# One batch's Newton steps on another engine, and tiles moved within the memory, in a fused attention and two-MLP kernel

## The chip, the cores and the metric

The kernel runs on one core of a Trainium2 chip. The metric is the device time of one execution in microseconds (us), from the first to the last instruction and what lies around it. Three executions of the kernel before took 1564.74, 1565.35 and 1567.13 us; their median is 1565.35 us.

## The reference

Three stages follow one another. Linear attention over 8 batches of 8 heads with 576 positions, each head divided by its root mean square; then an MLP with a cosine gate; then an MLP whose two halves are multiplied.

```python
kv  = einsum('bhsd,bhse->bhde', k, v)
out = einsum('bhsd,bhde->bhse', q, kv)
out = out / sqrt(mean(out * out, -1) + 1e-6) * g_norm
x = out laid out as 4608 tokens x 512
h = x @ w_in                  # 512 -> 2048
x = (h * cos(h)) @ w_out      # 2048 -> 512
h = ((x @ w1) * (x @ w2)) @ w3
y = h @ w_out                 # 1024 -> 512
```

Everything is float32. The kernel keeps the precision by splitting each operand into a high and a low part and multiplying three times (high by high, high by low, low by high).

## The kernel before

**Units.** The attention is cut into 16 units of 288 positions, two to a batch. A unit needs, for each of four pairs of heads, a split of q into high and low (`emit_qs`, tile `hl`: the high half on ScalarE, the low half on VectorE for units 0 to 3 and on GpSimd from unit 4 on, see `small`), three matmuls (`emit_out`), and two reads of the result out of PSUM. Then come the mean squares (`emit_ms`) and the inverse root: `emit_rs` writes the sums to DRAM and reads them back into 128 x 18 (tile `rsx`), `emit_newton` finds the root with a seed and three Newton rounds, 11 small instructions on VectorE, `emit_bc` writes it to DRAM and reads it back spread over the partitions (tile `bc`, one buffer), and `emit_x` multiplies. For units 2 and 3 (the second batch) all these transfers are issued from GpSimd's queue (`queue`); for the later units from SyncE's.

**First MLP.** Tokens go in blocks of 512. A step n multiplies a block with one of 16 weight pairs: `emit_h` (12 matmuls, PSUM tile `h`), the gate (`g_first`, `g_rest`: ScalarE and VectorE in turns, tile `g`), and two steps later `emit_w` (12 matmuls into tile `x`). Steps 0 to 7 take block 0, which needs units 0 and 1; step 8 starts block 1, which needs units 1, 2 and 3. So units 2 and 3 are worked out while steps 0 to 6 run (the table `quick`), and while the weights that arrive are unpacked on VectorE and ScalarE (`bits`, `Pair`). Later units are spread over later steps (`unit_stage`).

**Second MLP.** `emit_wc` folds two weight matrices into one (tile `wc`), then chains of products with 384 columns (tiles `X`, `V`, `Y`, line 790) and the output matmuls with 512 columns (`emit_o`, tile `o`) run to the end.

**Order.** The instructions of an engine start in a fixed order. A planner sets that order when the program is built, from the order of the code, the dependences and a simulated timeline, and pulls work forward where an engine seems free: in the trace units 4 and 5 are worked on from 83 us, far ahead of the steps that they are written beside. `tc.issue_after(ins)` puts every instruction of its block that is on the engine of `ins` behind `ins` in that order.

**Where tiles lie.** A partition's memory is filled from both ends. On the left, in this order, are the pools `const` (`kv0` to `kv3`, `sel`, `gneg`, `spread`), `mlp` (rows, x, g) and `attn`, later `mlp2` (wo2, wc). On the right, down from the top at byte 221152, lie the weights, later the pool `right` (xc, w12, ab, some of wo2). In the program before, `spread` takes 384 bytes at byte 20768, the pool `mlp` begins at byte 21152, x at 31392 and g at 47776; weight 0 begins at 212960. All these operands have sizes and inner offsets that are multiples of 512 bytes where TensorE reads them, so two numbers describe them: 160, the place of the left ones within 512 bytes, and 480, that of the right ones. In `emit_h`, `emit_w` and `emit_o` the operand that streams through (512 columns) lies on the left and the stationary one on the right. In `emit_wc` the stationary one lies on the left, and the streaming one on the left for c below 4 and on the right from c = 4 on. In line 790 both lie on the right.

Of the kernel before, what the change touches and what calls it, by code (L numbers as in the profile page):

```python
# [7 lines left out]
F32 = mybir.dt.float32  # L8
F32R = mybir.dt.float32r
I32 = mybir.dt.int32  # L10
AF = mybir.ActivationFunctionType
ALU = mybir.AluOpType

P = 128
EPS = 1e-6
# [5 lines left out]
RSQRT_SEED = float(0x5F3759DF)  # L21
HUGE = 3.0e38
# [7 lines left out]
def f32(ap):  # L30
    return ap.bitcast(F32)
# [3 lines left out]
def kernel(  # L35
# [18 lines left out]
    nc = tc.nc  # L54
    B, NPAIR, NHALF, _, HALF = qt.shape
# [10 lines left out]
    RS = 2 * NPAIR * HALF // P  # L66

    const = ctx.enter_context(tc.tile_pool(name="const", bufs=1))
    wstack = ExitStack()
    wpool = wstack.enter_context(tc.tile_pool(name="weights", bufs=1, side="right"))  # L70
    dram = ctx.enter_context(tc.tile_pool(name="scratch", bufs=1, space=bass.MemoryType.DRAM))
# [5 lines left out]
    ap = attn.enter_context(tc.tile_pool(name="attn", bufs=1))  # L77
# [11 lines left out]
    load = {"vector": 0.0, "pool": 0.0, "alone": True}  # L89

    def even(n):

        if load["alone"]:
            return nc.vector
        v, g = load["vector"] + 60 + n * 1.05, load["pool"] + 100 + n * 1.8
        if v <= g:
            load["vector"] = v
            return nc.vector
        load["pool"] = g
        return nc.gpsimd  # L100

    def split(dst, src, lo_engine=None):

        nc.scalar.activation(dst[:, 0], src, AF.Copy)  # L104
        lo_engine = lo_engine or even(src.shape[-1])
        lo_engine.tensor_tensor(dst[:, 1], src, f32(dst[:, 0]), ALU.subtract)  # L106
# [174 lines left out]
    def queue(u):  # L281

        return nc.gpsimd if 2 <= u < 4 else nc.sync

    def small(u):
        return None if u < 4 else nc.gpsimd

    q_raw = {}
# [9 lines left out]

    def emit_qs(u, p):
        hl = ap.tile([P, 2, HALF], F32R, tag="hl", bufs=2, name=f"qhl_{u}_{p}")  # L300
        split(hl, q_raw.pop((u, p)), small(u))
        q_hl[p] = hl

    o_sb = {}
# [44 lines left out]
    def newton(x, y, t):  # L349

        nc.vector.tensor_scalar(
            y.bitcast(I32), x.bitcast(I32), -0.5, RSQRT_SEED, ALU.mult, ALU.add
        )
        for _ in range(3):
            nc.vector.tensor_tensor(t, x, y, ALU.mult)
            nc.vector.scalar_tensor_tensor(t, t, 0.5, y, ALU.mult, ALU.mult)
            end = nc.vector.scalar_tensor_tensor(y, t, 1.5, y, ALU.subtract, ALU.mult)
        return end

    def emit_newton(u):  # L360

        x = rs[u]
        y, t = (
            ap.tile([P, RS], F32, tag=f"rs{i}", bufs=2, name=f"rs{i}_{u}") for i in range(2)
        )
        load["vector"] += 1000
        nc.vector.tensor_scalar(x, x, EPS, HUGE, ALU.add, ALU.min)
        newton(x, y, t)
        rs[u] = y

    bc = {}

    def emit_bc(u):
        y = rs.pop(u)
        d = dram.tile([2 * NPAIR, HALF], F32, tag="rsd", bufs=2, name=f"rsd_{u}")
        queue(u).dma_start(out=d.rearrange("h s -> (h s)").rearrange("(p f) -> p f", f=RS), in_=y)
        t = ap.tile([P, NPAIR, HALF], F32, tag="bc", name=f"bc_{u}")
        rows = d.rearrange("(p h) s -> h p s", h=2)
        for h in range(2):
            queue(u).dma_start(out=t[64 * h:64 * h + 64], in_=rows[h].partition_broadcast(64))  # L380
        bc[u] = t

    def emit_x(u, p):
# [6 lines left out]
    T3 = HALF // NT3  # L390
# [81 lines left out]
    def unit_stage(u, s, newton=NEWTON, last=LAST):  # L472
# [16 lines left out]
        if 1 <= s <= NPAIR:  # L489
            late.append(lambda: emit_qs(u, s - 1))  # L490
# [6 lines left out]
        if s == newton:  # L497
            late.append(lambda: emit_newton(u))
            late.append(lambda: emit_bc(u))
# [387 lines left out]
    if True:  # L887
# [5 lines left out]
        nc.gpsimd.memset(sel, 0.0)  # L893
        for h in range(2):
            nc.gpsimd.memset(sel[D * h:D * h + D, h:h + 1], 1.0 / D)
        spread = const.tile([P, T3], F32, name="spread")
        nc.gpsimd.memset(spread, 0.0)
        nc.gpsimd.affine_select(
            out=spread, in_=spread, compare_op=ALU.not_equal, fill=1.0, base=0,
# [12 lines left out]
        for h in range(2):  # L912
            nc.sync.dma_start(
                out=gneg[D * h:D * h + D], in_=g_norm.rearrange("(d o) -> d o", o=1)
# [32 lines left out]
        for n in range(NS + 2):  # L947
            t, m, first, last = steps[n] if n < NS else (NB, n - NS, False, False)
# [171 lines left out]
        h, g = order[-1]  # L1120
# [63 lines left out]
```

## Time and profile before

| what | value |
|---|---|
| median of three executions | 1565.35 us |
| the profiled execution | 1564.83 us |
| its span, first to last instruction | 1563.0 us |
| TensorE busy | 1517.0 us (97%), 7616 matmuls |
| VectorE, ScalarE, GpSimd busy | 921.4, 694.0, 370.9 us |
| mean granted TensorE clock | 0.991 of full speed |

The profile is of one execution. A matmul's end is modelled, so the rate at which matmuls follow each other is read from their starts. Times inside the trace count from the first instruction; 1.8 us lie outside the span.

### The profile page before, as it was taken

How to read it: one execution, taken by the hardware profiler on the slowest of the kernel's cores; microseconds unless marked ns; L12 is line 12 of the kernel's file. 1: busy time of each engine (PE TensorE's matmuls, PEld its weight loads, DVE VectorE, ACT ScalarE, POOL GpSimd, SP SyncE). 2: the span in 40 equal slices, each digit the busy share in tenths (PEclk: the TensorE clock that was granted, in tenths of full speed). 3: DMA queues.
4: the chain of work that ended last, by engine and by line, in shares of the span. 5: the costliest groups of instructions: out<-in, count | busy, mean ns of one | idle time of the engine just before them, and what ended most of it. 6: DMA issues, size and time to landing. Idle time of an engine off the chain costs nothing.

```text
span 1563.0 us, 20358 instructions
## 1 busy us (share of the span) xinstructions
PE 1517.0 (97%) x7616; PEld 1271.9 (81%) x7616; DVE 921.4 (59%) x1639; ACT 694.0 (44%) x1375; POOL 370.9 (24%) x301
## 2 busy tenths in 40 slices
PE   6887999999999999999999998999999999999998
PEld 6665888777787787777878786989998898999997
DVE  4986774567566676656665546745434456545453
ACT  5665554444444454444534335443333334333331
POOL 1121020011010121101102005464344416444420
PEclk9898999999999999999999999999999999999999
DMA  9653020433423424334222106121112313233312
GB/s 347 217 175 88 0 78 21 147 99 94 123 85 122 128 96 132 97 118 132 84 65 81 46 0 229 41 68 68 44 65 82 108 37 116 75 111 121 122 60 75
DMA packets 79794, 156.24 MB, mean 100 GB/s; under 512 B 11360, under 2 KB 37136, under 8 KB 77776
## 3 DMA queue, kind: packets, MB, share of 16 engines
q1 hardware_dynamic: 78080, 150.18, 29.3%
q0 software_dynamic: 1616, 4.78, 0.9%
q8 instruction: 59, 0.97, 0.3%
q14 instruction: 39, 0.32, 0.1%
HBM read 113.77 MB, written 41.15 MB: 99 GB/s over the span
## 4 chain that ended last, share of the span: by engine, by line
PE 82%; DMA 6%; POOL 4%; DVE 3%; ACT 2%; issue 2%; SPq 1%; ACTq 0%; DVEq 0%; POOLq 0%
PE X L790 10%; PE h L555 8%; PE h L556 8%; PE h L557 8%; PE x L557 8%; PE x L556 8%; PE x L555 8%; PE V L790 5%; PE o L555 4%; PE o L556 4%; PE o L557 4%; PE Y L790 2%; POOL xc L106 2%; DMA x2r<-x_all 2%; DMA words<-in_w1pair_dram 2%
## 5 line engine op out<-in xcount | busy, mean ns | idle before, releaser
L790 PE MATMUL X<-xc,w 128*128 128x384 f32 x1152 | 229.5, 337 | 6.5 <-ACT s L798 5.8
L556 PE MATMUL x<-g,w 128*128 128x512 f32 x576 | 229.4, 398 | 1.1 <-DVE g L106 1.1
L557 PE MATMUL x<-g,w 128*128 128x512 f32 x576 | 229.2, 398 | 0.0
L555 PE MATMUL h<-x,w 128*128 128x512 f32 x544 | 219.2, 404 | 9.7 <-DVE u L583 5.0
L790 PEld LDWEIGHTS X<-xc,w 128*128 128x128 f32 x1152 | 203.7, 188 | 20.3 <-ACT s L798 9.9
L556 PE MATMUL h<-x,w 128*128 128x512 f32 x544 | 217.9, 400 | 0.0
L557 PE MATMUL h<-x,w 128*128 128x512 f32 x544 | 217.3, 399 | 0.0
L555 PE MATMUL x<-g,w 128*128 128x512 f32 x576 | 210.5, 397 | 2.5 <-ACT g L104 2.5
L106 POOL TENSOR_TENSOR xc<-x2r,xc 128x768 fp32r<-128x768 f32 x70 | 133.3, 1911 | 227.3 <-ACT xc L104 227.3
L569 ACT ACTIVATE u<-h 128x512 f32<-128x512 f32 x144 | 86.1, 598 | 178.7 <-PE h L557 175.4
L582 ACT ACTIVATE u<-u 128x512 f32<-128x512 f32 x144 | 90.8, 631 | 115.6 <-DVE u L578 104.0
L106 DVE TENSOR_TENSOR g<-u,g 128x512 fp32r<-128x512 f32 x144 | 103.8, 721 | 63.8 <-ACT g L104 63.5
L104 ACT ACTIVATE g<-u 128x512 fp32r<-128x512 f32 x144 | 91.0, 632 | 101.3 <-DVE u L583 75.3
L555 PEld LDWEIGHTS h<-x,w 128*128 128x128 f32 x544 | 103.5, 191 | 39.6 <-DVE u L583 8.7
L556 PEld LDWEIGHTS x<-g,w 128*128 128x128 f32 x576 | 108.8, 189 | 27.9 <-DVE g L106 1.9
L577 DVE TENSOR_SCALAR r<-u 128x512 f32<-128x512 f32 x112 | 51.1, 456 | 136.3 <-ACT u L569 135.9
L555 PEld LDWEIGHTS x<-g,w 128*128 128x128 f32 x576 | 107.6, 188 | 28.1 <-ACT g L104 2.9
L557 PEld LDWEIGHTS x<-g,w 128*128 128x128 f32 x576 | 108.8, 189 | 25.8
L106 POOL TENSOR_TENSOR qhl<-q,qhl 128x288 fp32r<-128x288 f32 x48 | 43.1, 900 | 360.3 <-ACT qhl L104 293.5
L798 ACT ACTIVATE s<-X 128x384 f32<-128x384 f32 x144 | 65.9, 487 | 134.0 <-PE X L790 133.8
L583 DVE TENSOR_TENSOR u<-u,h 128x512 f32<-128x512 f32 x144 | 98.4, 683 | 44.5 <-ACT u L582 44.1
L557 PEld LDWEIGHTS h<-x,w 128*128 128x128 f32 x544 | 103.6, 191 | 24.5 <-issue 0.5
(185 smaller groups left out, 2629.4 us busy)
## 6 DMA issues: line engine op xcount, KB each, us to landing
x2r<-x_all SPq DMA_DIRECT2D x44, 384.0 KB
words<-in_w1pair_dram SPq DMA_DIRECT2D x15, 1024.0 KB
kvraw<-in_kv_main_dram SPq DMA_DIRECT2D x28, 512.0 KB
x_all<-x2s SPq DMA_DIRECT2D x36, 256.0 KB
part<-o SPq DMA_DIRECT2D x36, 256.0 KB
part<-part SPq DMA_DIRECT2D x36, 256.0 KB
out_dram<-part SPq DMA_DIRECT2D x36, 256.0 KB
d_w<-in_w12w_dram SPq DMA_DIRECT2D x16, 512.0 KB
```

What stands on the lines that cost most here:

```text
L104: nc.scalar.activation(dst[:, 0], src, AF.Copy)
L106: lo_engine.tensor_tensor(dst[:, 1], src, f32(dst[:, 0]), ALU.subtract)
L555: nc.tensor.matmul(ps, w[0], x[0], start=first, stop=False)
L556: nc.tensor.matmul(ps, w[0], x[1], start=False, stop=False)
L557: nc.tensor.matmul(ps, w[1], x[0], start=False, stop=last)
L569: nc.scalar.activation(u, h_ps[n], AF.Identity, bias=0.25, scale=INV_2PI)
L577: nc.vector.tensor_scalar(r, u, ROUND, ROUND, ALU.add, ALU.subtract)
L582: nc.scalar.activation(u, u, AF.Sin, scale=-TWO_PI_DOWN)
L583: nc.vector.tensor_tensor(u, u, h_ps.pop(n), ALU.mult)
L790: nc.tensor.matmul(ps, w[:, self.i, a, k], x[:, b, k], start=first and k == 0 and n == 0, stop=last and k == 1 and n == 2, skip_group_chec ...
L798: nc.scalar.activation(s, ps, AF.Copy)
```

## The change

The Newton steps of units 2 and 3 move from VectorE to GpSimd. `newton_on_gpsimd` spells out in 13 instructions what took 10, as the fused form (two operations with two tensors) is split; with the clamp in `emit_newton` it is 14 instead of 11. The low halves of units 4 and 5 are put behind the last transfer of unit 3's spreading in GpSimd's order. `spread` moves from the pool `const` into the slot of `bc`, which leaves the left side 384 bytes shorter ahead of the pool `mlp`. A tile of 48 floats that nothing reads or writes is placed first on the right side, so that all behind it lies 192 bytes lower.

```diff
     const = ctx.enter_context(tc.tile_pool(name="const", bufs=1))
+
+    shift = ctx.enter_context(tc.tile_pool(name="shift", bufs=1, side="right"))
+    shift.tile([P, 48], F32, name="shift")
@@
-        split(hl, q_raw.pop((u, p)), small(u))
+        with tc.issue_after(spreads[0].ins) if u in (4, 5) else nullcontext():
+            split(hl, q_raw.pop((u, p)), small(u))
@@
+    def newton_on_gpsimd(x, y, t):
+        nc.gpsimd.tensor_scalar(
+            y.bitcast(I32), x.bitcast(I32), -0.5, RSQRT_SEED, ALU.mult, ALU.add
+        )
+        for _ in range(3):
+            nc.gpsimd.tensor_tensor(t, x, y, ALU.mult)
+            nc.gpsimd.tensor_tensor(t, t, y, ALU.mult)
+            nc.gpsimd.tensor_scalar(t, t, 0.5, -1.5, ALU.mult, ALU.add)
+            nc.gpsimd.tensor_tensor(y, t, y, ALU.mult)
@@
-        load["vector"] += 1000
-        nc.vector.tensor_scalar(x, x, EPS, HUGE, ALU.add, ALU.min)
-        newton(x, y, t)
+        engine = nc.vector
+        if 2 <= u < 4:
+            engine = nc.gpsimd
+        else:
+            load["vector"] += 1000
+        engine.tensor_scalar(x, x, EPS, HUGE, ALU.add, ALU.min)
+        (newton if engine is nc.vector else newton_on_gpsimd)(x, y, t)
@@
+        if u == 3:
+            spreads.append(op)
@@
-        spread = const.tile([P, T3], F32, name="spread")
+        spread = ap.tile([P, T3], F32, tag="bc", name="spread")
```

## Rows read from the trace of the kernel before

**Rows 1.** The page's first line.

```profile
span 1563.0 us, 20358 instructions
```

**Rows 2.** Busy time by stretch: PE, PEld, DVE, ACT, POOL, granted clock, DMA.

```profile
100.00:150.00 50.00, 36.67 (x167) 25.20 (x166) 31.66 (x81) 28.12 (x64) 10.57 (x14) 0.83 0.41 124
150.00:250.00 100.00, 100.00 (x429) 80.38 (x428) 69.73 (x97) 56.91 (x91) 8.50 (x8) 1.00 0.13 39
```

**Rows 3.** Chain that ended last, in order of time: start us, us, what.

```profile
93.44 4.98 DMA msd<-ms_sb
...
98.97 4.58 DMA rsx<-msd
...
121.42 4.55 DMA bc<-rsd
```

**Rows 4.** Timeline of DVE: start us, us, instruction, idle before and its releaser.

```profile
98.97 0.17 DVE L356 SCALAR_TENSOR_TENSOR rs<-rs,rs 128x18 f32<-128x18 f32 x1
103.57 0.18 DVE L367 TENSOR_SCALAR rsx<-rsx 128x18 f32<-128x18 f32 x1 [4.43 <-DMA rsx<-msd]
...
104.98 0.17 DVE L357 SCALAR_TENSOR_TENSOR rs<-rs,rs 128x18 f32<-128x18 f32 x1
...
126.00 1.56 DVE L386 TENSOR_TENSOR o<-o,bc 128x288 f32<-128x288 f32 x4 [6.47 <-DMA bc<-rsd]
```

**Rows 5.** Timeline of POOL, the same columns.

```profile
24.34 0.19 POOL L419 TENSOR_TENSOR gate<-sq 128x1 f32<-128x1 f32 x1 [21.83 <-ACT sq L413]
...
83.12 0.98 POOL L106 TENSOR_TENSOR qhl<-q,qhl 128x288 fp32r<-128x288 f32 x1 [4.24 <-ACT qhl L104]
89.40 3.51 POOL L106 TENSOR_TENSOR qhl<-q,qhl 128x288 fp32r<-128x288 f32 x1 [5.30 <-DVE rs L355]
92.85 1.18 POOL L345 DMA_DIRECT2D msd<-ms_sb  x2
...
118.46 0.59 POOL L376 DMA_DIRECT2D rsd<-rs  x1 [0.70 <-DVE rs L357]
120.81 1.23 POOL L380 DMA_DIRECT2D bc<-rsd  x2 [1.77 <-DMA rsd<-rs]
...
135.03 0.81 POOL L106 TENSOR_TENSOR qhl<-q,qhl 128x288 fp32r<-128x288 f32 x1 [4.18 <-ACT qhl L104]
```

**Rows 6.** Timeline of PE where block 1 begins.

```profile
126.88 1.22 PE L555 MATMUL h<-x,w 128*128 128x512 f32 x2 [2.49 <-ACT x L104]
...
141.58 0.50 PE L555 MATMUL h<-x,w 128*128 128x512 f32 x1 [4.86 <-DVE u L583]
```

**Rows 7.** Timeline of PE, first MLP: streaming left, stationary right.

```profile
750.09 0.40 PE L555 MATMUL x<-g,w 128*128 128x512 f32 x1
...
755.69 0.40 PE L555 MATMUL x<-g,w 128*128 128x512 f32 x1
```

**Rows 8.** Timeline of PE, `emit_wc` with c below 4: both on the left.

```profile
948.87 0.39 PE L555 MATMUL wc<-wo,w3hl 128*128 128x512 f32 x1
...
954.31 0.39 PE L555 MATMUL wc<-wo,w3hl 128*128 128x512 f32 x1
```

**Rows 9.** Timeline of PE, `emit_wc` with c from 4: streaming right, stationary left.

```profile
992.71 0.39 PE L555 MATMUL wc<-wo,w3hl 128*128 128x512 f32 x1
...
995.46 0.33 PE L790 MATMUL X<-xc,w 128*128 128x384 f32 x1
```

**Rows 10.** Timeline of PE, line 790: both on the right, 384 columns.

```profile
1007.26 2.24 PE L790 MATMUL X<-xc,w 128*128 128x384 f32 x12
1009.34 1.20 PE L790 MATMUL Y<-xc,w 128*128 128x384 f32 x6
```

**Rows 11.** PE by line, 150 to 1005 us: count, busy us, mean ns, idle before.

```profile
L557 PE MATMUL x<-g,w 128*128 128x512 f32 x543 | 215.3, 397 | 0.0
...
L557 PE MATMUL h<-x,w 128*128 128x512 f32 x497 | 196.5, 395 | 0.0
...
L557 PE MATMUL h<-x_again,w 128*128 128x512 f32 x32 | 12.7, 396 | 0.0
```

**Rows 12.** PE by line, 1005 to 1563 us, the same columns.

```profile
L790 PE MATMUL X<-xc,w 128*128 128x384 f32 x1118 | 222.3, 337 | 6.4 <-ACT s L798 5.8 <-DVE w L106 0.5
...
L557 PE MATMUL o<-wchl,ab 128*128 128x512 f32 x288 | 110.5, 394 | 0.0
```

More of the change, by code (lines that the diff above doesn't have):

```diff
@@ L365, in emit_newton @@
         )
-        load["vector"] += 1000
-        nc.vector.tensor_scalar(x, x, EPS, HUGE, ALU.add, ALU.min)
-        newton(x, y, t)
+        engine = nc.vector
[5 more added lines that the diff above has]
+        (newton if engine is nc.vector else newton_on_gpsimd)(x, y, t)
         rs[u] = y
     bc = {}
+    spreads = []
     def emit_bc(u):
@@ L379, in emit_bc @@
         for h in range(2):
-            queue(u).dma_start(out=t[64 * h:64 * h + 64], in_=rows[h].partition_broadcast(64))
+            op = queue(u).dma_start(
+                out=t[64 * h:64 * h + 64], in_=rows[h].partition_broadcast(64)
+            )
+        if u == 3:
+            spreads.append(op)
         bc[u] = t
```

## Prediction

> **What bounds the kernel now.** I read the busy time by stretch first. From 150 us on TensorE is busy without a gap at full clock, and it stays so until the second MLP, where single waits of the products add up to 6.4 us [rows 2, 12]. The one long stretch in which it idles is 100 to 150 us: busy for 36.67 of 50 us, at a mean clock of 0.83 [rows 2]. So two things can move the end: when block 1 starts, and how fast matmuls follow each other afterwards.
>
> For the first, the chain of waits from 93 to 126 us is read. It hardly touches TensorE; it is unit 3's inverse root on its way through DRAM: the sums out (4.98 us), back in (4.58), Newton, the root out, and the spread copy in (4.55) [rows 3]. VectorE shows what else this costs. It had all but the end of unit 2's root at 98.97, then stood 4.43 us at unit 3's first small instruction, whose data were still under way, and gave out unit 2's last step at 104.98 [rows 4]. Unit 3's root was finished 14.9 us after its data came (103.57 to GpSimd's write at 118.46) [rows 4, 5], though each step takes 0.17 us, since they are queued between large instructions. Block 1's first matmul is at 126.88, behind the product with `bc` at 126.00 [rows 4, 6].
>
> For the second, the timeline of TensorE is read by starts. 24 matmuls of the first MLP take 755.69 - 750.09 = 5.60 us, 233.3 ns each [rows 7]. 24 of `emit_wc` with the same shape take 954.31 - 948.87 = 5.44 us, 226.7 ns each, while both operands lie on the left [rows 8]. From c = 4 on, 12 take 995.46 - 992.71 = 2.75 us, 229.2 ns [rows 9]. The engine, the shape, the clock and the instruction pair are the same; what differs is where the operands lie. In line 790, with 384 columns and both operands on the right, one takes (1009.34 - 1007.26) / 12 = 173.3 ns [rows 10]. The two rates whose operands have the same place within 512 bytes (160 with 160, 480 with 480) differ by 53.4 ns for 128 columns: 0.417 ns a column, one cycle of the full clock of 2.4 GHz, and 13.3 ns on top of the columns for each. By the same measure 480 with 160 has 15.9 on top and 160 with 480 has 20.0.
>
> **The change, the places.** Left tiles behind `const` move down by 384 bytes: 160 becomes 288 (160 - 384 + 512). Right tiles move down by 192: 480 becomes 288. After the change the streaming and the stationary operand of every large matmul have the same place. The trace shows no pair at 288; I take the value of the two equal pairs, 226.7 ns, as they are the only rows with equal places and agree on both sides of the memory. The bounds are 226.7 and 233.3 (nothing happens); no row is slower than 233.3. The gain is 6.67 ns a matmul. In the first MLP after 150 us each of the three lines has about 543 + 497 + 32 = 1072 [rows 11], so 3216 x 6.67 ns = 21.4 us; TensorE had no wait there and VectorE was busy 70% [rows 2], so all of it counts. The output matmuls, 3 x 288 = 864 [rows 12], lie on left and right as the first MLP's do: 864 x 6.67 = 5.8 us, of which I take 5.5, as ScalarE already kept the products waiting for 5.8 us [rows 12] and could again. `emit_wc` gains below 0.3 us, line 790 nothing. Together 27 us, between 0 and 27.
>
> The Trainium skill speaks against this term: its page "TensorE: Matmul & The Clock Gate", Part 2, says that TensorE reads the streaming and the stationary operand through two independent ports, so that loading the next weights takes no bandwidth from the running matmul, and gives 215.8 ns for 512 columns. By that the places would not matter and the term would be 0; the starts above, 226.7 to 233.3 ns by place, do not agree with it.
>
> **The change, the start of block 1.** Removed from VectorE are 22 small instructions and the stand of 4.43 us. That shortens nothing by itself: TensorE has work for steps 5 to 7 either way and must then wait for unit 3. The new path runs on GpSimd, in order: unit 2's 14 instructions from the landing at about 83, its write and spread, unit 3's sums out and in, its 14 instructions, its write and spread.
>
> The price of a small GpSimd instruction is not in the trace. Below it is bounded by the 128x1 product, 0.19 us; 128x288 takes 0.81 undisturbed, so 128x18 should take 0.23 [rows 5]. Above, the disturbed ones: 0.98 beside a large VectorE instruction and once 3.51 [rows 5], so 0.2 to 2.7 us of waiting each. 14 instructions cost 3.2 us alone, and at about one VectorE instruction of 0.5 us each, 14 x 0.73 = 10. VectorE is full around 85 us and less so after 105, so I take 10 us for unit 2 and 6 for unit 3.
>
> This waiting is the rule of the skill's page "SBUF — State Buffer", section "SBUF: two separate sides": VectorE and GpSimd share a pair of ports, which one instruction holds to its end. The trace agrees (0.81 against 0.98 and 3.51).
>
> The sum: 83 + 10 = 93; unit 2's write, its landing and its spread 0.59 + 1.76 + 1.23 = 3.6 (unit 3's pieces from 118.46 to 122.04) [rows 5], 96.6; unit 3's sums out to the read's issue 98.97 - 92.85 = 6.1, in 4.6, so 107.3 [rows 3, 5]; Newton 6, 113.3; write and spread 126.0 - 118.5 = 7.5 [rows 4, 5]: 120.8 instead of 126.0, 5 us earlier. If the planner puts unit 3's sums ahead of unit 2's spread it is 3 to 4 us better; undisturbed (3.2 us each) the sums go at about 90.7 and block 1's data land at 112.7, 13 us earlier. With twelve more microseconds of waiting it is later than now.
>
> What is late next: the refill. After block 1's first two steps TensorE stood 4.86 us for the gate [rows 6]; that stays. Units 4 and 5 leave the gap that they fill today: 24 short matmuls and 8 sums, some 5 us of TensorE work, of which part can run while unit 3's spread is under way and part inside the 4.86 us. I put this at 0 to 3 us, set against the clear queue ahead of block 1, and take 0 for both. Queued behind the waiting: GpSimd's low halves of units 4 and 5 hold the q buffers, so SyncE's q loads of these units wait some 30 us longer (the first such half runs at 83 now and could at about 116 then), and the weight words queued behind them with those; block 1 needs the next weights from step 16, 45 us after its start, which hides it. If that cover failed it would show as a wait of ScalarE for words. `spread` in the slot of `bc` and the empty tile cost no instruction: `spread` is read for the last time before unit 2 begins. Their only effect is the places. The start is worth 5 us, between 13 gained and 6 lost.
>
> **Sum.** 27 + 5 = 32 us off the profiled 1564.83 (span 1563.0 [rows 1] and 1.8 around it): 1532.8. The median is 0.5 above that execution, so 1533.
>
> **Rivals.** (1) The places do nothing: the same four numbers also fit "operands on the same side are fast, on two sides slow", since no row has equal places on two sides. Then only the start is left, 1565 - 5 = 1560. For it: the pages' rule above, and that a place within 512 bytes is my reading of four pairs. Against it: 16 for right with left and 20 for left with right need the order of the places too. The chance is 0.17. (2) Slower: the places do nothing and the port decides. If each of the 28 GpSimd instructions costs over 0.76 us, unit 3's spread lands later than today (120.8 - 16 = 104.8 without the Newtons, and 126.0 - 104.8 = 21.2 for 28). The mechanism is one wait on VectorE before each dependent instruction; at the mean waiting of the two disturbed rows (0.17 and 2.70, so 1.43 us) in half of them, 28 x (0.23 + 0.72) = 26.6 us, it lands at 131.4, and with units 4 and 5 out of the gap (3 us) the time is 1565 + 5 + 3 = 1573. The chance is 0.08. (3) A middle: equal places at 288 give the 229.2 of rows 9 and not 226.7: 4080 x 4.1 ns = 16.7, with the start 1543; it is within my forecast's range.
>
> **How the numbers follow.** Forecast 0.75, with 1521 to 1545 as its own range (places 17 to 27 us, start 13 gained to 6 lost). No pair at 288 was seen, so the range has to reach into rival 1: 1521 to 1558 leaves out rival 2 and half of rival 1, about 0.17, plus a little at the ends. A measurement of this kernel tells about 0.2%, 3 us, from no change. Faster by more: all of the forecast and 0.12 of rival 1, 0.87. Within it 0.06, slower 0.07.
>
> **What would show it.** Right: starts of 24 matmuls of the first MLP 5.44 us apart; the 226.7 ns in `emit_o` too; line 790 at 173.3 as now; no small inverse-root instruction of units 2 and 3 on VectorE and no 4.43 us stand there; the product with unit 3's `bc` near 121; GpSimd's small instructions at 0.2 to 1.0 us. Wrong: 5.60 us per 24 as now (rival 1); a rate above that; GpSimd's Newton over 10 us for each unit; TensorE standing at a matmul of unit 4 while work of steps 6 or 7 is ready; ScalarE waiting for words after block 1 has begun.

## The result, and the profile after

The changed kernel takes **1551.65 us** (median of four executions, 1548.50 to 1553.01), the kernel before 1565.05 (four, 1564.56 to 1567.13). The ratio is 0.9909, with a 95% interval from 0.9891 to 0.9927. The change gains 13.4 us where 32 were forecast: the time lies within the whole range given (1521 to 1558), but outside the likeliest case's own (1521 to 1545). The profiled execution took 1550.75 us, 14.1 less than that of before.

The page's first line and busy time by stretch (us; then busy time and count for PE, PEld, DVE, ACT and POOL; granted clock of TensorE; DMA share; GB/s), as [rows 1, 2]:

```profile
span 1549.0 us, 20361 instructions
...
100.00:150.00 50.00, 33.75 (x145) 24.06 (x146) 28.30 (x58) 24.68 (x58) 20.31 (x30) 0.76 0.37 107
150.00:250.00 100.00, 99.58 (x443) 81.20 (x442) 72.26 (x109) 59.30 (x98) 10.44 (x10) 1.00 0.14 42
```

From 150 to 250 us TensorE now starts 443 matmuls, where it started 429: they follow each other faster. In the stretch from 100 to 150 us, where the Newton steps were to help, it is busy for less time than before (33.75 us for 36.67), at a lower mean granted clock (0.76 of the full 2.4 GHz for 0.83; the two levels are 1.2 and 2.4 GHz).

The timeline of TensorE shows the rate, as [rows 7]. The two starts below are 24 matmuls of the first MLP apart; then come the first of a run of four output matmuls and the product behind it; then two waits:

```profile
735.62 0.39 PE L579 MATMUL x<-g,w 128*128 128x512 f32 x1
741.06 0.39 PE L579 MATMUL x<-g,w 128*128 128x512 f32 x1
...
1211.09 0.39 PE L579 MATMUL o<-wchl,ab 128*128 128x512 f32 x1
...
1212.01 1.21 PE L814 MATMUL X<-xc,w 128*128 128x384 f32 x6
```

```profile
612.86 0.69 PE L274 MATMUL kv<-kvraw 128*64 128x64 f32 x16 [1.11 <-DMA kvraw<-in_kv_main_dram]
...
851.32 0.50 PE L579 MATMUL h<-x,w 128*128 128x512 f32 x1 [1.53 <-DVE u L607]
```

(741.06 - 735.62) / 24 = 226.7 ns: the forecast rate exactly. The four output matmuls take 0.92 us, 230 ns each, and not 226.7. And TensorE, whose longest wait between 150 us and the folded weights was 0.4 us before, now has two of over 1 us: for VectorE's gate at 851, for a transfer at 613.

GpSimd's timeline (start, us, instruction, idle before and its releaser), as [rows 5]. First unit 2's root and transfers, then unit 3's:

```profile
80.83 4.03 POOL L386 TENSOR_SCALAR rsx<-rsx 128x18 f32<-128x18 f32 x1 [1.65 <-DMA rsx<-msd]
84.94 0.21 POOL L366 TENSOR_SCALAR rs<-rsx 128x18 int32<-128x18 int32 x1
85.23 5.89 POOL L370 TENSOR_TENSOR rs<-rsx,rs 128x18 f32<-128x18 f32 x1
91.20 0.23 POOL L371 TENSOR_TENSOR rs<-rs,rs 128x18 f32<-128x18 f32 x1
...
95.70 0.61 POOL L396 DMA_DIRECT2D rsd<-rs  x1 [0.29 <-POOL rs L373]
100.71 1.26 POOL L400 DMA_DIRECT2D bc<-rsd  x2 [4.40 <-DMA rsd<-rs]
101.96 1.19 POOL L350 DMA_DIRECT2D msd<-ms_sb  x2
106.69 0.57 POOL L351 DMA_DIRECT2D rsx<-msd  x1 [3.53 <-DMA msd<-ms_sb]
108.67 0.94 POOL L386 TENSOR_SCALAR rsx<-rsx 128x18 f32<-128x18 f32 x1 [1.42 <-DMA rsx<-msd]
...
118.59 0.62 POOL L396 DMA_DIRECT2D rsd<-rs  x1 [0.29 <-POOL rs L373]
120.94 1.25 POOL L400 DMA_DIRECT2D bc<-rsd  x2 [1.74 <-DMA rsd<-rs]
```

A small instruction costs 0.21 to 0.23 us when nothing is in its way, but two of unit 2's took 4.03 and 5.89. Unit 3's sums go out at 101.96, against 92.85 before, since they stand behind unit 2's spread; its root is written at 118.59, against 118.46. The trip of these sums to DRAM and back is shorter than before, though: 6.71 us from the first issue to the first instruction of the root (101.96 to 108.67), against 10.72 (92.85 to 103.57).

VectorE and TensorE at the same time, as [rows 4, 6]:

```profile
94.13 0.23 DVE L109 TENSOR_TENSOR kv<-kv,kv 64x64 fp32r<-64x64 f32 x1
105.81 1.56 DVE L410 TENSOR_TENSOR o<-o,bc 128x288 f32<-128x288 f32 x4 [11.45 <-DMA bc<-rsd]
107.29 0.68 DVE L109 TENSOR_TENSOR g<-u,g 128x512 fp32r<-128x512 f32 x1
...
126.24 1.57 DVE L410 TENSOR_TENSOR o<-o,bc 128x288 f32<-128x288 f32 x4 [5.91 <-DMA bc<-rsd]
```

```profile
108.03 0.79 PE L580 MATMUL x<-g,w 128*128 128x512 f32 x1 [8.39 <-DVE g L109]
...
109.05 0.63 PE L580 MATMUL x<-g,w 128*128 128x512 f32 x1
109.47 0.63 PE L581 MATMUL x<-g,w 128*128 128x512 f32 x1
...
127.12 1.22 PE L579 MATMUL h<-x,w 128*128 128x512 f32 x2 [2.75 <-ACT x L107]
```

VectorE stands 11.45 us at the product with unit 2's spread. Behind that product in its order is step 5's split of g (107.29), and TensorE stands 8.39 us for it. Behind that stand its clock is at the lower level: matmuls follow each other every 0.42 to 0.43 us and not every 0.227. Unit 3's product comes at 126.24, not at 120.8; block 1 starts at 127.12, as late as before.

### The profile page after: what moved, and what is told of

The parts are those of the page before. It is cut to its first block, busy times and chain, and to the rows that moved or that the text cites. A ratio compares the mean times of both kernels' runs of the same rounds, so it can differ in the third digit from the quotient of the medians.

```text
span 1549.0 us, 20361 instructions
## 1 busy us (share of the span) xinstructions
PE 1496.2 (97%) x7616; PEld 1272.9 (82%) x7616; DVE 917.2 (59%) x1617; ACT 692.5 (45%) x1375; POOL 389.9 (25%) x329
## 4 chain that ended last, share of the span: by engine, by line
PE 79%; DMA 8%; DVE 4%; POOL 4%; ACT 2%; issue 1%; SPq 1%; ACTq 0%; POOLq 0%; DVEq 0%
PE X L814 11%; PE h L579 8%; PE h L580 8%; PE h L581 8%; PE x L581 7%; PE x L580 7%; PE x L579 7%; PE V L814 5%; PE o L579 4%; PE o L580 4%; PE o L581 4%; PE Y L814 3%; POOL xc L109 2%; DMA x2r<-x_all 2%; DMA words<-in_w1pair_dram 2%
## 5 line engine op out<-in xcount | busy, mean ns | idle before, releaser
L580 PE MATMUL x<-g,w 128*128 128x512 f32 x576 | 226.6, 393 | 10.8 <-DVE g L109 10.8
L581 PE MATMUL x<-g,w 128*128 128x512 f32 x576 | 226.7, 394 | 0.0
L579 PE MATMUL h<-x,w 128*128 128x512 f32 x544 | 216.6, 399 | 8.0 <-ACT x L107 4.2
L580 PE MATMUL h<-x,w 128*128 128x512 f32 x544 | 214.5, 394 | 0.0
L581 PE MATMUL h<-x,w 128*128 128x512 f32 x544 | 213.8, 393 | 0.0
L579 PE MATMUL x<-g,w 128*128 128x512 f32 x576 | 208.6, 391 | 0.1
```

What stands on the lines that cost most here:

```text
L579: nc.tensor.matmul(ps, w[0], x[0], start=first, stop=False)
L580: nc.tensor.matmul(ps, w[0], x[1], start=False, stop=False)
L581: nc.tensor.matmul(ps, w[1], x[0], start=False, stop=last)
```

## The experiments

Two questions were open: which part of the change brought how much, and through what the Newton steps on GpSimd lost time. The record of the first four speaks of a theory A (the places carry the gain, and the rest of the change loses) with two forms for the loss: A1, units 4 and 5 held back, and A2, the Newton steps on GpSimd. Beside the first four the kernel before took 1565.09 us; beside the fifth to eighth 1565.19; beside the last two 1566.28.

**The places alone.**

```diff
+    shift = ctx.enter_context(tc.tile_pool(name="shift", bufs=1, side="right"))
+    shift.tile([P, 48], F32, name="shift")
-        spread = const.tile([P, T3], F32, name="spread")
+        spread = ap.tile([P, T3], F32, tag="bc", name="spread")
```

> The kernel before with the places alone: the added tile moved out of the constants and the empty 192 bytes on the right, Newton steps and order as before. Theory A (the whole gain comes from the places, and the move of the Newton steps costs about 3 us at the start of block 1): 24 matmuls of the first MLP in 5.44 us, block 1's first matmul at 127 as before, step 12 no later than before (154.4), the end 17 us earlier: 1547 to 1549 us, so 3 us faster than the whole change. Rival B (the engine's move gives a part of the 13.4 us): slower than the whole change, 1553 to 1556. Rival C (the two are independent and the start costs nothing in the median): the same as the whole change, 1551 to 1552.

Measured: 1546.57 us (1544.93 to 1547.83), ratio 0.9878 [0.9863, 0.9892]. The places bring 18.5 us by themselves, more than the whole change (theory A, 0.4 us below its range). The order of instructions is that of before on every engine, so nothing else can have.

**The rest alone**: the change without these four lines.

> The change without the places: Newton steps of units 2 and 3 on GpSimd, units 4 and 5 behind them, the added tile in the constants and no empty tile. The order on every engine is that of the whole change. Theory A: 24 matmuls in 5.60 us as before, GpSimd's two Newtons over 20 us together, step 12 some 3 us later than before, 1567 to 1569 us. Rival B: 1558 to 1563, faster than before. Rival C: 1564 to 1566.

Measured: 1568.35 us (1566.33 to 1571.52), ratio 1.0021 [1.0009, 1.0032]. The Newton steps on GpSimd and the holding back cost 3.3 us together. This is the sign that the forecast had wrong.

**The places and the Newton steps, without the holding back of units 4 and 5.**

```diff
-        with tc.issue_after(spreads[0].ins) if u in (4, 5) else nullcontext():
-            split(hl, q_raw.pop((u, p)), small(u))
+        split(hl, q_raw.pop((u, p)), small(u))
```

> The whole change without the holding back of units 4 and 5: their low halves stand in GpSimd's order wherever the planner puts them. Theory A1 (the 3 us at the start are units 4 and 5 put out of the gap ahead of block 1): step 12 at 154 to 155, 1547 to 1549 us. Rival A2 (the 3 us are GpSimd's Newton itself, which ends as late as VectorE's did and holds up VectorE at the product with unit 2's spread): step 12 at 157 or later, 1551 to 1554 us.

Measured: 1553.29 us (1549.36 to 1554.67). Without the holding back the Newton steps lose 6.7 us (1553.29 - 1546.57). With the Newton steps on GpSimd the holding back itself brings 1.6 us (1553.29 - 1551.65), which the spread of the executions doesn't tell from nothing.

**The places and the holding back, with the Newton steps on VectorE.**

```diff
-        if 2 <= u < 4:
-            engine = nc.gpsimd
-        else:
-            load["vector"] += 1000
+        load["vector"] += 1000
```

> The whole change with the Newton steps back on VectorE: units 4 and 5 still behind unit 3's spread in GpSimd's order, places as in the change. Theory A1 (units 4 and 5 put out of the gap cost the 3 us): step 12 at 157, 1550 to 1552 us. Rival A2 (GpSimd's Newton costs them): step 12 at 154 to 155 and 1547 to 1549 us.

Measured: 1543.24 us (1542.27 to 1544.73), ratio 0.9858 [0.9843, 0.9872]; repeated on another chip beside the fifth to seventh, 1543.29. Both theories had expected more (1547 or above).

> The fourth experiment's kernel once more, beside the three others on one chip, so that they are compared with it directly: places and the holding back, with both Newtons on VectorE. 1543 us, within 2 us.

So A1 falls: with the Newton steps on VectorE the holding back gains 3.3 us (1546.57 - 1543.24). A2's sign holds, not its size: the Newton steps on GpSimd lose 8.4 (1551.65 - 1543.24). GpSimd's timeline of this kernel, then VectorE's two products, show what the kernel after lacks:

```profile
90.24 1.17 POOL L350 DMA_DIRECT2D msd<-ms_sb  x2 [11.40 <-ACT kv L107]
94.19 0.57 POOL L351 DMA_DIRECT2D rsx<-msd  x1 [2.77 <-DMA msd<-ms_sb]
101.26 0.56 POOL L393 DMA_DIRECT2D rsd<-rs  x1 [6.50 <-DVE rs L356]
104.67 1.26 POOL L397 DMA_DIRECT2D bc<-rsd  x2 [2.85 <-DMA rsd<-rs]
114.54 0.56 POOL L393 DMA_DIRECT2D rsd<-rs  x1 [8.61 <-DVE rs L362]
```

```profile
110.13 1.56 DVE L407 TENSOR_TENSOR o<-o,bc 128x288 f32<-128x288 f32 x4 [2.21 <-DMA bc<-rsd]
...
122.16 1.19 DVE L407 TENSOR_TENSOR o<-o,bc 128x288 f32<-128x288 f32 x3 [7.92 <-DMA bc<-rsd]
```

Unit 3's sums go out at 90.24, as soon as they are there, with no low half of unit 4 ahead of them (3.51 us long in [rows 5], with the sums at 92.85 behind it): that is where the holding back gains. And unit 2's spread is issued later than in the kernel after (104.67 against 100.71), yet VectorE stands only 2.21 us for it, since work of steps 5 to 7 stands ahead of the product here.

**One unit at a time.** The Newton steps of unit 2 alone on GpSimd (the diff), then those of unit 3 alone (`u == 3`); the rest as in the kernel after.

```diff
-        if 2 <= u < 4:
+        if u == 2:
```

> The kernel after, but unit 3's Newton steps are back on VectorE; unit 2's stay on GpSimd. Theory P (place in the queue): the loss against the version with both on VectorE (1543.2 us) comes from unit 2, whose 14.6 us on GpSimd push its own spread from about 93 to 100.7 us and, behind it in GpSimd's order, unit 3's sums from 90.2 to 102.0 us. Then this kernel keeps most of the loss, 1549 to 1552 us, and unit 3's sums still go at about 102. Rival W (the waiting of small instructions adds up, whichever unit): the loss of 8.4 us is shared as the steps' times, 14.6 and 9.6 us, so this kernel keeps 5 us of it: about 1548, and the next one 1546.5.

> The kernel after, but unit 2's Newton steps are back on VectorE; unit 3's stay on GpSimd. Theory P: unit 3's sums go at about 90 us again, its root is done on an engine with nothing else to do by 110 us, and the time is that of the version with both on VectorE or better: 1540 to 1544 us. Rival W: unit 3's part of the waiting stays as a loss: about 1546.5 us.

Measured: 1548.07 us (1546.92 to 1551.34) with unit 2, 1542.91 (1541.68 to 1544.25) with unit 3. The first is rival W's figure (1548) and a little below theory P's range (1549 to 1552), so it doesn't tell them apart; the second does. Unit 3's steps on GpSimd alone cost nothing, where rival W had 1546.5; unit 2's alone cost 4.8 us (1548.07 - 1543.29). The two don't add up to the 8.4 of both. Theory P's mechanism shows in GpSimd's timelines: with unit 2 there (first line) unit 3's sums go at 102.52; with unit 3 there (the others) at 90.20, and its root is done by 109.05.

```profile
102.52 1.20 POOL L350 DMA_DIRECT2D msd<-ms_sb  x2
```

```profile
90.20 1.17 POOL L350 DMA_DIRECT2D msd<-ms_sb  x2 [11.53 <-ACT kv L107]
...
109.05 0.60 POOL L396 DMA_DIRECT2D rsd<-rs  x1 [0.29 <-POOL rs L373]
```

The other 3.6 us between unit 2 alone and both are not explained by the start of block 1, which is even later with unit 2 alone (130.70 against 127.12). At step 128 (841 us) the two kernels are 1 us apart; the wait of 1.53 us at 851 is in the kernel after and not in the other. At the end the profiled executions are 2.7 us apart. Why both cost more than unit 2 alone stays open.

**Two ways to take the loss away, one by one and together.** The first sends unit 3's sums by SyncE's queue, so that they don't stand behind unit 2's root. The second puts VectorE's product with unit 2's spread behind step 6's gate in VectorE's order. The Newton steps of both units stay on GpSimd.

```diff
+        q = nc.sync if u == 3 else queue(u)
         for h in range(2):
-            queue(u).dma_start(out=rows[h], in_=m[h:P:32])
+            q.dma_start(out=rows[h], in_=m[h:P:32])
```

> The kernel after, but unit 3's sums go out and come back by SyncE's queue instead of GpSimd's, so they no longer stand behind unit 2's root and spread. They should go out at about 91 us and be back by 100, and GpSimd begins unit 3's root as soon as it has issued unit 2's spread, at 102 instead of 108.7. If unit 3's lateness decides when block 1 begins, its spread lands some 6 us earlier, and the time falls to about 1545 to 1547 us. If unit 2's late spread decides (VectorE stood 11.45 us for it and TensorE 8.39 behind that), nothing is gained: 1550 to 1552 us.

```diff
+        with tc.issue_after(gates[6].ins) if u == 2 else nullcontext():
-        engine.tensor_tensor(o, o, bc[u][:, p, :], ALU.mult)
+            engine.tensor_tensor(o, o, bc[u][:, p, :], ALU.mult)
...
-            5: [(2, 10), (3, 8)], 6: [(3, 10)],
+            5: [(3, 8)], 6: [(2, 10), (3, 10)],
```

> The kernel after, but VectorE's product with unit 2's spread is put behind step 6's gate multiplication in VectorE's order (it stood ahead of step 5's split of g, and everything behind it waited 11.45 us for the spread). GpSimd's order is untouched, so unit 2's spread still lands at 105.8 us and unit 3's product still comes near 126. Theory O (the order on VectorE, not the length of the root, costs the time): TensorE's stand of 8.39 us at step 5's g falls below 3 us, steps 5 and 6 end some 8 us earlier, and of the 8.4 us that the move lost 3 to 5 come back, as block 1 still waits for unit 3: 1546.5 to 1549 us. Rival L (unit 3's lateness alone decides): 1550 to 1552 us, as after.

> Both repairs at once: the product with unit 2's spread behind step 6's gate on VectorE, and unit 3's sums by SyncE's queue. Both Newtons stay on GpSimd. If these two together are the whole loss of the move, the time is that of the version with both Newtons on VectorE, 1542 to 1545 us. If the small instructions' own time on GpSimd is a cost beside them, it stays at 1546 to 1549.

Measured: 1548.04 us (1542.62 to 1555.03, a wide spread) with the sums by SyncE; 1549.38 (1546.88 to 1549.76) with the later product; **1541.75** (1533.32 to 1543.67), ratio 0.9835 [0.9809, 0.9861], with both. The first two fall between what their theories gave, and neither settles anything alone: 3.6 and 2.3 us come back, and with the later product TensorE's stand at step 5's g is gone, but it stands 4.43 us at step 6's. Together 9.9 come back, all that the move had lost; by the medians that is more than the sum of the two, but the spread of the first is too wide to be sure. Each cause hides behind the other: with the sums early, VectorE still stood 11.44 us for unit 2; with the product later, unit 3's root still came at 118.78. With both, GpSimd's second root (first and last of its 14 instructions), VectorE's two products and TensorE's longest stand read:

```profile
103.04 0.29 POOL L387 TENSOR_SCALAR rsx<-rsx 128x18 f32<-128x18 f32 x1
...
107.05 0.22 POOL L374 TENSOR_TENSOR rs<-rs,rs 128x18 f32<-128x18 f32 x1
```

```profile
108.85 1.56 DVE L412 TENSOR_TENSOR o<-o,bc 128x288 f32<-128x288 f32 x4 [7.98 <-DMA bc<-rsd]
...
119.97 1.57 DVE L412 TENSOR_TENSOR o<-o,bc 128x288 f32<-128x288 f32 x4
```

```profile
114.66 0.79 PE L583 MATMUL x<-g,w 128*128 128x512 f32 x1 [10.28 <-DVE g L109]
```

Unit 3's product is at 119.97, 6 us earlier than before, and block 1 starts at 121.68. The root took 107.27 - 103.04 = 4.2 us, while VectorE stood still beside it. VectorE's stand of 7.98 us is still there; step 5's gate is ahead of it now, but step 6's split of g is behind it, and TensorE stands 10.28 us for that one, longer than in the kernel after. What is smaller is the sum of the stands, and above all the time at the lower clock. Counted from the first matmul of step 6 (`h`) to the first of step 24, in one execution each:

| kernel | whole, us | TensorE idle, us | TensorE busy at 1.2 GHz, us |
|---|---|---|---|
| the kernel after | 136.5 | 17.0 | 17.3 |
| the places alone | 131.2 | 13.3 | 13.5 |
| places and holding back, Newton on VectorE | 129.3 | 11.3 | 13.9 |
| the same on the other chip | 130.8 | 13.4 | 12.5 |
| both repairs | 127.7 | 13.7 | 5.9 |

A matmul takes nearly twice as long at the lower clock (0.43 us for 0.227), so 47% of the last column is lost. Between the kernel after and the one with both repairs that is 5.4 us, and the stands are 3.3: together 8.7 of 8.8. So in this execution most of what comes back is the clock: the lower level lasted from 107.4 to 117.6 us, mostly inside the long stand (104.4 to 114.7). Against the versions with the Newton steps on VectorE the loss is mostly stands: 3.6 to 5.7 us of them, and some 1.6 to 2.3 of clock. The two executions of one kernel show how far a single trace can be trusted here: they are 1.5 us apart. This version is as fast as the one with both Newton steps on VectorE, or a little faster; their values overlap.

**What place means.** Four kernels with the right side alone shifted, the left as before: by 320 bytes (80 floats, the diff), 128, 64 and 192. The times are of one execution each.

```diff
+    shift = ctx.enter_context(tc.tile_pool(name="shift", bufs=1, side="right"))
+    shift.tile([P, 80], F32, name="shift")
```

> The kernel before with an empty tile of 320 bytes first on the right side, so the right operands lie at 160 within 512 bytes, as the left ones do (160). Theory D (only the two operands' relative place counts): matmuls of the first MLP follow each other every 226.7 ns, and the time is that of the places alone, 1545 to 1549 us. Rival S (288 is a good place by itself): 229 to 233 ns, 1555 to 1566 us.

> The kernel before with an empty tile of 128 bytes first on the right: the right operands lie at 352, the left at 160, so the stationary one of the first MLP lies 192 bytes behind the streaming one (modulo 512). In the kernel before it is 320, and 192 in the second half of the folded weights, at 229.2 ns. Theory D: 229.2 ns here too, and the time about 1555 us. If the sides count beside the place: not 229.2.

> The kernel before with an empty tile of 64 bytes first on the right: right operands at 416, a distance of 256 bytes to the left ones. Theory D gives no value between the measured ones but bounds: 229.2 ns (distance 192) to 233.3 (distance 320), some 1555 to 1565 us. If the distance counts from either side (256 is the largest), 233.3 or above.

> The kernel before with an empty tile of 192 bytes first on the right: right operands at 288, left at 160, distance 128. This is the right half of the change without the left half. Theory D: between the 226.7 ns of distance 0 and the 229.2 of distance 192, so 226.7 to 229.2, and 1546 to 1555 us. If the left half were what matters: 233.3 and 1565 us.

Two starts, 24 matmuls of the first MLP apart, in the kernels with 320, 128, 64 and 192 bytes:

```profile
735.30 0.39 PE L558 MATMUL x<-g,w 128*128 128x512 f32 x1
740.74 0.39 PE L558 MATMUL x<-g,w 128*128 128x512 f32 x1
```

```profile
736.73 0.39 PE L558 MATMUL x<-g,w 128*128 128x512 f32 x1
742.22 0.39 PE L558 MATMUL x<-g,w 128*128 128x512 f32 x1
```

```profile
735.74 0.39 PE L558 MATMUL x<-g,w 128*128 128x512 f32 x1
741.17 0.39 PE L558 MATMUL x<-g,w 128*128 128x512 f32 x1
```

```profile
737.05 0.40 PE L558 MATMUL x<-g,w 128*128 128x512 f32 x1
742.65 0.40 PE L558 MATMUL x<-g,w 128*128 128x512 f32 x1
```

| place right - left, modulo 512 | ns a matmul | time, us |
|---|---|---|
| 0 (320 bytes; 160 and 160) | 226.7 | 1547.00 |
| 0 (the kernel after; 288 and 288) | 226.7 | (other edits too) |
| 192 (128 bytes) | 228.9 | 1553.79 |
| 256 (64 bytes) | 226.7 | 1544.51 |
| 128 (192 bytes) | 233.3 | 1564.52 |
| 320 (the kernel before) | 233.3 [rows 7] | 1564.83 |

That 288 is no special place follows from the first two lines; that the place of the right operand alone doesn't decide follows from 288 on the right, 226.7 with 288 on the left and 233.3 with 160. In all the pairs seen the distance decides, and 192 gives in the first MLP what it gave in `emit_wc` (229.2, [rows 9]) with the sides exchanged. But the steps between were wrong: 256 is as fast as 0, against both bounds written down for it, and 128 is as slow as 320. Fast are the two distances that are multiples of 256; other distances were not tried. The change's right half alone is the kernel with 192 bytes: it gains nothing without the left half.

## Why the prediction was partly right and partly wrong

**The places: the mechanism was right, the price too high (27 us for 18.5).** The rate of 226.7 ns was forecast and came. Rival 1, that places do nothing, is out. So is what the prediction drew from the Trainium skill's page "TensorE: Matmul & The Clock Gate", Part 2 (loading weights takes no bandwidth from the running matmul), that the places would not matter: a shift of 64 bytes on one side changes the rate from 233.3 to 226.7. Whether it is the loading of weights that the distance acts on was not tested. But 27 us was the term, and the places alone bring 18.5 (17.7 between the profiled executions).

*The first MLP* was to bring 3216 x 6.67 = 21.4 us. From the first matmul of step 12 to the last of this MLP the kernel with the places alone gains 16.8 us (154.43 to 945.89 before, 153.07 to 927.75 there). The wrong step is "TensorE had no wait there, so all of it counts". It multiplied the clean rate with every matmul. In the stretch from 200 to 860 us the spacings below 260 ns average 227.2 for 233.3 there: 6.2 and not 6.67, as behind each interruption by kv, out or ms the matmuls run at 228 to 236 first: two or three behind most of the out, four to six behind kv and ms. That makes 19.9. And a stage without waits has them once the engine that sets its pace is faster: 1.54 us for VectorE's gate at 846, 0.8 more for transfers of k and v (1.2 for 0.4); the spacings above 300 ns rise from 24 to 29 in that stretch, and what they have above 227 from 2.6 to 5.1 us.

*The output matmuls* were to bring 5.5 us; the stretch behind the folded weights, which holds them, gained 1.0. The step "lie on left and right as the first MLP's do" was right, but they come in runs of 1 to 24 between products (54 at the end), and the clean rate is reached late in a run: 230 ns in the four shown, 228.4 in the runs of 24. All their spacings average 229.8 ns, and 232.4 before, so they gained 2.2 us. Against before, the kernel with the places alone leads by 18.1 us at the last matmul of the first MLP, by 16.7 behind the folded weights, which wait for VectorE's `w3hl` and give 1.4 us back, and by 17.7 at the last output matmul. Half of the 2.2 went where the prediction had seen that some could go, into the products' waits, most of them for ScalarE: 7.4 us for 6.4 [rows 12] in the kernel with the places alone (988 to 1546 us):

```profile
L793 PE MATMUL X<-xc,w 128*128 128x384 f32 x1120 | 222.6, 337 | 7.4 <-ACT s L801 6.9 <-DVE w L109 0.5
```

**The start of block 1: the sign was wrong.** Forecast was 5 us gained; the kernel after loses 5.1 against the places alone (5.3 from step 6 to step 24 of the traces: 3.7 of stands, some 1.8 of clock). Three steps failed.

*The root's time.* 10 us were taken for unit 2 and 6 for unit 3; they took 14.6 (80.83 to 95.41) and 9.6 (108.67 to 118.29). The undisturbed price was right (0.21 to 0.23 us, 4.2 for a root that VectorE left alone). The waiting was mis-sized: about one VectorE instruction of 0.5 us was assumed for each. Twice a GpSimd instruction was passed by a train. During the 5.89 us VectorE ran six large instructions back to back (the last below), and GpSimd's ended at 91.12, during a small one behind them that reads PSUM:

```profile
89.83 1.21 DVE L164 TENSOR_TENSOR w<-words,w 128x1024 fp32r<-128x1024 f32 x1
90.96 0.20 DVE L109 TENSOR_TENSOR kv<-kv,kv 64x64 fp32r<-64x64 f32 x1
```

The trace of before had shown such a train: the instruction of 3.51 us at 89.40 [rows 5] waited 2.70 us, longer than VectorE's longest beside it, which took 1.21:

```profile
91.00 1.21 DVE L161 TENSOR_TENSOR w<-words,w 128x1024 fp32r<-128x1024 f32 x1
```

Ports that one instruction holds to its end do not by themselves give 2.70 us there, so the trace agreed less than the prediction said. Rival 2's price for the port, 26.6 us for 28 instructions, was the better one: they took 24.2, over the 21.2 from which the prediction has unit 3 later than today. So the sum's 96.6 for the end of unit 2's spread issue became 101.97.

*What stands behind it.* The prediction listed unit 3's sums behind unit 2's spread in GpSimd's order and gave 3 to 4 us if they stood ahead. It priced the landing of unit 2's root at 1.76 us, from unit 3's in [rows 5]; it was waited for 4.40. So the sums went at 101.96 instead of 96.6, and unit 3's spread was issued at 120.94 instead of 115.7 (113.3 for the root and 2.35 from its write to the spread [rows 5]). That it was no worse is luck: the root began at 80.83 and not at 83, and the sums' trip out and in took 6.7 us and not 10.7. These two hide 6.2 us of the mis-sized terms.

*What stands behind unit 2's spread on VectorE.* This was not in the prediction at all, and the repairs speak for it: with the sums early, putting the product later takes the median from 1548.04 to 1541.75, though their values just overlap. "Removed from VectorE are 22 small instructions and the stand of 4.43 us" treats the stand as gone. It moved: the product with unit 2's spread was put ahead of step 5's split of g, and stood for 11.45 us. TensorE paid 8.39 of it, at a time when the prediction had it at work on steps 5 to 7 "either way". It was queued behind the very root that had moved. The removed instructions were worth little: in the version that keeps them on VectorE, a large instruction behind one of them starts 0.07 to 0.09 us after it.

**Units 4 and 5: taken as 0, worth 3.3 us with the Newton steps on VectorE.** The two effects that were set against each other are not equal there. Of their 24 short matmuls 18 come behind block 1's start, and 3 before the holding back, and the clear queue lets unit 3's sums go 2.3 us earlier and its root 2.8 (92.49 to 90.24 and 117.36 to 114.54, from the places alone to the places with the holding back). With the steps on GpSimd, as forecast, 0 was not far off (1.6 us, not told from nothing).

The sum by the profiled executions: the places fall 9.3 us short, the rest 8.6 (5 forecast gained, 3.6 lost at the end of the trace against the places alone). That is the whole difference between 1532.8 and 1550.75.

**The range.** The likeliest case's own range does not follow from the parts given with it: 17 to 27 us for the places and 13 gained to 6 lost at the start give 1525 to 1554 and not 1521 to 1545, and 1551.65 lies in that. The wider range held the time because it reached for rival 1, not for what happened. The limits given for the start don't follow either: the undisturbed case adds up to 111.2 (83 + 3.2 + 3.6 + 6.1 + 4.6 + 3.2 + 7.5) and not 112.7, and from the 16 us taken for the two roots 5.2 more, not twelve, make unit 3 later than before.

## What to carry to other kernels

When work moves to another engine, follow both sides: what stands behind it in the new engine's order, and which instruction on the old engine waits for its result and what stands behind that one. Price a faster rate by the spacing of all matmuls, with what restarts and short runs take, and ask which engine is late once the first one is faster. Where both operands of a matmul come from memory at fixed places, try a few shifts of one side: here 64 bytes alone gave about 20 us. And judge a stand of TensorE by what runs at the lower clock behind it, not by its length alone.

## What the runs showed of the hardware

- With these shapes the spacing of matmuls depends on the distance of the two operands' places: 226.7 ns at 0 and 256 bytes, 228.9 at 192, 233.3 at 128 and 320. Why is open.
- A GpSimd instruction of 0.22 us can take 5.89 us beside VectorE. Four kernels show it (5.89 to 5.90 each, with 4.00 to 4.03 for the first instruction of unit 2's root, which starts at 80.6 to 81.8 us). In the kernel with the later product alone the same root starts at 82.06 and none of its instructions takes over 1.07; without the holding back it starts at 80.46 and none takes over 1.09. With the same order but the old places the two took 4.02 and 2.42. What lets a train pass was not tested. The Trainium skill's page "SBUF — State Buffer" (section "SBUF: two separate sides") says that the pair of ports is held to the end of one instruction; if these are waits for that pair, one through six instructions shows that the one that waits isn't always next.
- A long stand of TensorE can be paid again in the clock: between 100 and 150 us the mean of its two levels, 1.2 and 2.4 GHz, was 0.76 of the upper one in the kernel after, busy for 33.75 us, and 0.86 in the one with the places alone, busy for 37.12; from 100 to 110 us, which hold most of the stand of 8.39 us, it was 0.63 and 0.83. How much is paid again differs: 17.3 us of work ran at the lower level between steps 6 and 24 in the kernel after, and 5.9 in the one with both repairs, which has the longest single stand.
